# A four-segment attention and feed-forward kernel: earlier loads and tile-by-tile statistics for the third segment, another place for two loads of ScalarE, and a new table of offsets

## The chip, the cores and the metric

The kernel runs on one core of a Trainium2 chip. The core has five engines, each with an instruction queue of its own that it works through in order: TensorE (PE) for matrix products, VectorE (DVE), ScalarE (ACT), GpSimd (POOL), and SyncE (SP), which here only issues DMA transfers. Engines wait for each other through semaphores. The metric is the time of one execution on the device in microseconds; several runs are taken, and their median is quoted.

## The reference

There are 2048 tokens of width 640, 32 heads of width 20, and four segments of 512 tokens. Two layers are computed, each an attention block and a feed-forward block, both behind a layer norm and with a residual sum:

```
x = x + A(layernorm(x))
x = x + B(layernorm(x))     # relu(x @ w1) @ w2, inner width 1728
x = x + A(layernorm(x))
x = x + B(layernorm(x))

A: q, k, v = x @ wq, x @ wk, x @ wv, for 32 heads and 4 segments
   for s in range(4):
       a_dot = softmax(q_s k_s^T * scale + causal mask) v_s
       a_mem = phi(q_s) M / (phi(q_s) z + 1e-6)
       out_s = g * a_mem + (1 - g) * a_dot,     g = sigmoid(beta)
       M, z  = M + phi(k_s)^T v_s, z + sum(phi(k_s))
   return concat(out) @ wo
```

The layer norm subtracts the mean of a token's 640 values and divides by the root of their variance plus 1e-5. Before a segment's q, k and v can be projected, the statistics of its four tiles of 128 tokens must be known.

## The kernel before

The program writes no instruction order by hand. Some forty generators (streams) each describe one strand of the work: scores, exps, the causal masks, the products with v, projections, layer norms, phi, the feed-forward block, loads. A planner (class Sched) runs while the program is built. It keeps a model of when each engine is free and when each result is there, asks every stream for its next operation, and appends the one that can start first to its engine's queue. The key by which it chooses is the start time plus an offset, then a priority, then the segment. The offset comes from the table SHIFT, whose entries (stream, segment from 0 to 7 over both layers, part) give nanoseconds, negative for earlier. Durations and latencies in `dve`, `act`, `pool`, `pe` and `dma` are the planner's estimates. They alter no instruction, only the order in which instructions are put into the queues. When the program runs on the chip, the order is fixed and the semaphores decide the times.

The data goes this way. For each segment the token tiles lie in x_sb (16 tiles, a place of its own for each). `stats` (L772) makes two bn_stats of 320 columns and one bn_aggr per tile on DVE; `chain` makes the inverse root on POOL (L791); `lnorm` (L801) writes normalized tiles (L821) and has SP transpose them by DMA (`turn`, L794) into xnT, or into a part of hT for the second and third segment of the first layer. Groups of matmuls (L754 in full form, L757 in four column quarters) make q, k and v. DVE or ACT evict them out of PSUM (L961 and L962 for q and k, L1016 for v). q and k go through DRAM (scr) into the padded layout `pad`, from which PE makes the scores (L1281). ACT takes their exponentials (L1345), POOL cuts them along the diagonal (L1357), PE multiplies them with v (L1377) and the result is evicted (L1387). The products with wo, a second layer norm and the feed-forward block follow, and fill PE between the rounds of scores.

The very first segment is special. Its four tiles are loaded by `loads` (L599): tiles 0 and 1 by SP, 2 and 3 by ACT, at the start of both queues. DVE makes the statistics of tiles 0 and 1, ACT those of tiles 2 and 3 (`first_ln_b`, L887: a sum and a sum of squares, L893 to L897). They are transposed on PE (L846). `consts` (L661) lets ACT run one small exp at the start, so that its table is loaded; the same generator later makes omg and maskg from beta. `warm_pe` keeps PE busy with matmuls that nobody reads (L718). The pads of the first two head groups don't go through DRAM: `first_heads` (L1055) copies them from stg with four DMAs on SP and five on ACT (L1077).

`late_loads` (L621) is a list of pieces that SP loads later: the third segment's four tiles (the segment called 2 in the code), wo in five rows, the fourth segment's tiles, w1 in halves and w2. Each piece waits for one of the rounds of exps: piece n of the first 23 for round n*19//23, counted in fives, and all for z1 (two memsets). A name has one semaphore, whose event is set when the last piece of that name has been issued. All four tiles of a segment have one name, and `proj_ln` (L910) waits for it ahead of all four.

Of the kernel before, what the change touches and what calls it, by code (L numbers as in the profile page):

```python
# [6 lines left out]
ACT = mybir.ActivationFunctionType  # L7
ALU = mybir.AluOpType
# [4 lines left out]
DH = 20  # L13
# [5 lines left out]
G = H // 4  # L19
# [90 lines left out]
class Op:  # L110
# [4 lines left out]
    def __init__(self, alts, waits, dma=None, acq=None, urgent=False, take=(), mode="full", lag=0.0, port=False):  # L115
        self.lag = lag
        self.port = port
        self.alts = alts
        self.mode = mode
        self.cols = None  # L120
        self.cols_ns = None
        self.acq = acq
        self.waits = [t for t in waits if t is not None]
        self.dma = dma
        self.urgent = urgent
        self.take = take

# [31 lines left out]
class Spawn:  # L159
# [1565 lines left out]
```

## Time and profile before

| what | value |
|---|---|
| median of 3 runs | 554.52 us (554.39 to 555.2) |
| the profiled execution | 554.0 us |
| its span, from first to last instruction | 551.5 us |
| PE busy | 540.9 us, 98% |
| DVE busy | 421.9 us, 77% |
| ACT busy | 409.5 us, 74% |
| POOL busy | 192.0 us, 35% |
| granted clock of PE | 1.000 |

Matmuls overlap in the array, and the profile gives each its whole length. So a stretch in which PE is busy all the time can still hold short gaps between matmuls that follow each other. Where PE's busy time falls below the length of a stretch, it stood idle for certain. Rows of waits have the engine, the line and tile that waited, what ended the wait, the total in us, the number of waits, and the longest. A name with q (SPq, ACTq) is that engine's queue of DMA issues.

### The profile page before, as it was taken

Reading aid. Unit: us, or ns where it says so; the run is one execution under the profiler, and the core shown is the slowest. Engines: PE = TensorE matmul, PEld = TensorE weight load, DVE = VectorE, ACT = ScalarE, POOL = GpSimd, SP = SyncE. Lnnn points to the kernel's source line nnn. Section 1 sums busy time; section 2 is a strip of 40 time slices with the busy share of each in tenths; the row PEclk is TensorE's granted clock in tenths of the full one; section 3 lists DMA queues with packets and bytes.
Section 4 is the critical chain, followed back from the end, with each engine's and each line's share of the span. In section 5 each row is a group of like instructions: output and inputs, shape, how many; then the busy total and the mean of one; then the engine's idle time right before and its main releaser. Section 6 shows DMA issues by size and latency. Waiting matters only on the chain.

```text
span 551.5 us, 20778 instructions
## 1 busy us (share of the span) xinstructions
PE 540.9 (98%) x9171; PEld 304.7 (55%) x9171; DVE 421.9 (77%) x1057; ACT 409.5 (74%) x526; POOL 192.0 (35%) x305
## 2 busy tenths in 40 slices
PE   8998999999999999999999999999999999999998
PEld 7542554455654556545555464554556655757656
DVE  5979998898888869977998888677797889537202
ACT  6799979889777877798788978888896788441140
POOL 5345354333243324444343434443433333301000
PEclk9999999999999999999999999999999999999999
DMA  8598999844455162543775524717186331440301
GB/s 274 147 185 243 214 177 194 240 96 85 125 102 130 45 144 69 93 105 75 132 134 110 100 40 122 134 45 117 23 155 177 73 50 34 91 77 15 88 2 51
DMA packets 133325, 62.21 MB, mean 113 GB/s; under 512 B 112116, under 2 KB 123124, under 8 KB 133236
## 3 DMA queue, kind: packets, MB, share of 16 engines
q1 hardware_dynamic: 132672, 60.36, 51.0%
q8 instruction: 72, 1.18, 0.9%
q10 hardware_dynamic: 564, 0.53, 0.3%
q14 instruction: 17, 0.14, 0.1%
HBM read 20.56 MB, written 12.85 MB: 61 GB/s over the span
## 4 chain that ended last, share of the span: by engine, by line
PE 87%; DVE 5%; ACT 3%; DMA 2%; SPq 1%; POOL 1%; issue 0%
PE ps L757 35%; PE ps L754 34%; PE ps L1281 8%; PE ps L1377 6%; ACT PT L1345 3%; PE ps L1160 2%; PE ps L1218 1%; DMA oT<-o_sb 1%; PE ps L1552 1%; DVE stats L775 1%; DVE xn_tok L821 1%; DMA pad<-scr 1%; POOL rstd L791 1%; DMA x_sb<-in_A_x_dram 1%; DVE otu L1387 0%
## 5 line engine op out<-in xcount | busy, mean ns | idle before, releaser
L1345 ACT ACTIVATE PT<-ps 128x1024 bf16<-128x1024 f32 x320 | 309.3, 1026 | 66.3 <-PE ps L1281 61.0
L1357 POOL TENSOR_SCALAR_AFFINE_SELECT PT<-PT 128x512 bf16<-128x512 bf16 x256 | 165.7, 665 | 244.0 <-ACT PT L1345 243.8
L757 PE MATMUL ps<-xnT,w_r 128*32 128x512 bf16 x1340 | 81.2, 379 | 0.0
L754 PE MATMUL ps<-w_r,hT 128*128 128x320 bf16 x428 | 69.1, 300 | 0.0
L1594 DVE TENSOR_TENSOR x_sb<-x_sb,ps 128x320 bf16<-128x320 bf16 (+1 forms) x65 | 30.9, 475 | 46.0 <-PE ps L757 41.5
L1281 PE MATMUL ps<-pad 20*128 20x512 bf16 (+3 forms) x1024 | 63.4, 301 | 1.8 <-ACT PT L1345 0.9
L757 PE MATMUL ps<-w_r,hT 128*32 128x320 bf16 (+1 forms) x1668 | 64.4, 295 | 0.0
L775 DVE BATCH_NORM_STATS2 stats<-x_sb 128x6 f32<-128x320 bf16 x124 | 55.4, 475 | 3.2 <-DMA x_sb<-in_A_x_dram 2.6
L754 PEld LDWEIGHTS ps<-w_r,hT 128*128 128x128 bf16 x428 | 39.5, 98 | 19.5 <-issue 5.0
L757 PEld LDWEIGHTS ps<-xnT,w_r 128*32 128x32 bf16 x1340 | 33.2, 97 | 30.7 <-issue 2.4
L757 PEld LDWEIGHTS ps<-w_r,hT 128*32 128x32 bf16 x1668 | 42.0, 97 | 12.9 <-issue 1.6
L1575 ACT ACTIVATE hT<-ps 128x512 bf16<-128x512 f32 x54 | 32.2, 598 | 20.7 <-PE ps L757 19.7
L1281 PEld LDWEIGHTS ps<-pad 20*128 20x128 bf16 x1024 | 17.8, 92 | 53.5 <-issue 25.0
L754 PE MATMUL ps<-xnT,w_r 128*128 128x512 bf16 x185 | 45.5, 380 | 0.0
L791 POOL TENSOR_TENSOR rstd<-lnU,mhalf 128x2 f32<-128x2 f32 (+2 forms) x27 | 20.9, 774 | 67.5 <-DVE lnU L787 65.3
L1499 DVE TENSOR_TENSOR x_sb<-x_sb,ps 128x320 bf16<-128x320 bf16 x64 | 30.0, 478 | 15.5 <-PE ps L757 12.7
L1377 PE MATMUL ps<-PT,v_aug 128*21 128x128 bf16 (+3 forms) x896 | 40.3, 300 | 0.0
L1387 DVE CAST otu<-ps 128x512 bf16<-128x512 f32 x48 | 32.6, 679 | 8.4 <-PE ps L1377 8.1
L1574 DVE TENSOR_SCALAR hT<-ps 128x512 bf16<-128x512 f32 x50 | 33.9, 680 | 5.4 <-PE ps L754 3.6
L961 DVE CAST stg<-ps 128x512 bf16<-128x512 f32 (+1 forms) x44 | 29.8, 677 | 9.6 <-PE ps L754 4.8
L757 PE MATMUL ps<-wo_r,oT 128*32 128x320 bf16 x896 | 35.5, 299 | 0.6 <-DMA oT<-o_sb 0.6
L821 DVE TENSOR_SCALAR xn_tok<-x_sb,mv,rstd 128x640 bf16<-128x640 bf16 x60 | 31.1, 550 | 5.1 <-POOL rstd L791 3.5
(117 smaller groups left out, 731.3 us busy)
## 6 DMA issues: line engine op xcount, KB each, us to landing
pad<-scr SPq DMA_DIRECT2D x124, 80.0 KB
scr<-stg SPq DMA_DIRECT2D x34, 256.0 KB, 3.0
out_dram<-x_sb SPq DMA_DIRECT2D x15, 160.0 KB, 1.8
w_r<-in_B_w_dram SPq DMA_DIRECT2D x10, 216.0 KB, 3.0
w_r<-in_B_w_dram SPq DMA_DIRECT2D x13, 160.0 KB, 3.0
x_sb<-in_A_x_dram SPq DMA_DIRECT2D x10, 160.0 KB, 3.7
scr<-w_r SPq DMA_DIRECT2D x5, 256.0 KB, 3.3
wv_r<-in_A_wv_dram SPq DMA_DIRECT2D x1, 800.0 KB, 8.7
```

What stands on the lines that cost most here:

```text
L754: return e.matmul(view(dst.ap, b), a, b, start=(k == 0), stop=(k == last))
L757: return e.matmul(view(dst.ap[rows], b), part, b, start=(k == 0), stop=(k == last))
L775: tk = yield dve(320, 1, lambda e, c2=c2: e.bn_stats(stats6[:, t, c2, :], x_sb[:, t, c2 * 320:(c2 + 1) * 320]), xt)
L821: nm = lambda e, bx, t, k: e.tensor_scalar(bx.ap[:, k * D:k * D + D], x_sb[:, t + k, :], mv[:, t + k, 0:1], rstd[:, t + k:t + k + 1], ALU. ...
L1281: fns.append([(lambda e, z=z, j=j, hh=hh, N=N, o=o, sl=sl, q=hh % 2: e.matmul(slot.ap[:, q, o:o + N], sl.ap[32 * hh:32 * hh + DH, z, 0, 12 ...
L1345: tx = yield act(1024, lambda e, dst=dst, src=src: e.activation(dst, src, ACT.Exp, scale=SCALE), sc + pw)
L1357: tm = yield pool(600.0, lambda e, reg=reg: e.affine_select(out=reg, in_=reg, pattern=[[0, 4], [1, 128]], compare_op=ALU.is_ge, fill=0.0, ...
L1377: fns.append((lambda e, OD, j=j, hh=hh: e.matmul(OD.ap[32 * hh:32 * hh + DH + 1, 128 * j:L], VAUG[vx(a, s)][:, j, 4 * g + hh, :], pt.ap[:, ...
L1387: te = yield evac(L, 1, lambda e: e.tensor_copy(dst, OD.ap), lambda e: e.activation(dst, OD.ap, ACT.Copy), [tk] + OTU[0].tks)
L1574: th = yield evac(512, 1, lambda e: e.tensor_scalar(hT[:, dc, :], bk.ap[:, :], 0.0, None, ALU.max), lambda e: e.activation(hT[:, dc, :], b ...
L1575: lambda e: e.activation(hT[:, dc, :], bk.ap[:, :], ACT.Relu), [tk] + HT.tks)
L1594: ta = yield dve(n, 1, lambda e: e.tensor_tensor(x_sb[:, t, c0:c0 + n], x_sb[:, t, c0:c0 + n], bk.ap[:, 0:n], ALU.add), [tk], urgent=True)
```

## The change

Five things change.

The pieces of the third and fourth segment's tiles get a name, a semaphore and an event for each tile, and `proj_ln` waits for tile i ahead of tile i's statistics.

The third segment's four pieces no longer wait for a round of exps or for z1: they come when `first_heads` has put its transfers into the queues. The other pieces keep their gates; the wait for z1 is taken up from the fifth piece on.

In `loads`, the loads of tiles 2 and 3 on ACT come after the small exp of `consts` in ACT's queue. That exp is preceded by the load of ACT's table.

In the planner, a DVE operation that shares a port with POOL is no longer held until POOL is free plus 150 ns. The planner now remembers the last operations of both engines, and lengthens one by the overlap with the other. The copy of omg and the products for maskg count as such operations. Latencies of some transfers are raised: 2700 for wk and wq in place of 2000, 2200 in place of 1500 for the first heads' pads, 2900 in place of 2400 for the transposes of o.

The table of offsets is another one: 267 entries before, 242 after, with one entry alike.

```
@@ SHIFT
-    (0, 0, 0): -201, (0, 7, 1): -12, (1, 0, 0): 400, (1, 0, 1): 400, (1, 0, 2): 400, (1, 1, 0): -275, (1, 1, 1): -225,
...
+    (1, 0, 0): -50, (1, 0, 1): -100, (1, 2, 0): 225, (1, 2, 1): 625, (1, 2, 2): 500, (1, 3, 0): 100, (1, 3, 1): -75,
...
@@ _alts
-            if e == "dve" and op.port and self.free["pool"] > start:
-                hold = max(hold, self.free["pool"] - start + PORT_NS)
+            if e == "dve" and op.port:
+                for a, b in self.held["pool"][-6:]:
+                    if a <= start + 66.0 < b:
+                        hold = max(hold, b - start + op.data - 70.0)
+            if e == "pool":
+                for a, b in self.held["dve"][-6:]:
+                    if a < start + hold and b > start:
+                        hold = hold + b - max(a, start)
@@ run
+            if e == "dve" and op.port:
+                self.held[e].append((end - op.data, end))
+            elif e == "pool":
+                self.held[e].append((start, end))
@@ ld
-            tk = yield dma(e, sem_("d_" + name), nbytes, fn, waits, lat=1470.0 if name[:2] == "x0" else 2000.0)
+            tk = yield dma(e, sem_("d_" + name), nbytes, fn, waits, lat=1470.0 if name[:2] == "x0" else 2700.0 if name[:2] in ("wk", "wq") else 2000.0)
@@ loads
             for t in range(4):
+                if t == 2:
+                    yield Need("warmed")
                 yield from ld(("sp", "act")[t // 2], "x0%d%d" % divmod(t, 2), 163840, lambda e, t=t: e.dma_start(
                     x_sb[:, t, :], xs[:, t, :]))
@@ late_loads
-                return [("x%d" % s, 163840, one(4 * s + i)) for i in range(4)]
+                return [("x%d%d" % (s, i), 163840, one(4 * s + i)) for i in range(4)]
...
-            z1 = yield Need("z1")
+            z1 = []
...
-                w = yield Need("ex", *divmod(25 + (n - n2) // 2 if n >= n2 else n * 19 // n2, 5))
+                if name[:2] == "x2":
+                    yield Need("direct", 0)
+                    w = []
+                else:
+                    w = yield Need("ex", *divmod(25 + (n - n2) // 2 if n >= n2 else n * 19 // n2, 5))
+                if n == 4:
+                    z1 = yield Need("z1")
@@ consts
-            yield act(4, lambda e: e.activation(warm[:], warm[:], ACT.Exp), [tw], psum=False)
+            ta = yield act(4, lambda e: e.activation(warm[:], warm[:], ACT.Exp), [tw], psum=False)
+            S.set("warmed", tks=[ta])
...
@@ proj_ln
-                xw = [[("x10",)]] * 2 + [[("x11",)]] * 2 if s == 1 else [[("x%d" % s,)]] * 4
+                xw = [[("x10",)]] * 2 + [[("x11",)]] * 2 if s == 1 else [[("x%d%d" % (s, i),)] for i in range(NJ)]
@@ first_heads
-                            sl.ap[p0:p0 + rb - ra, z], stg[ra - 128 * c:rb - 128 * c, c]), ev + sl.tks, issue=720.0, rate=200.0)
+                            sl.ap[p0:p0 + rb - ra, z], stg[ra - 128 * c:rb - 128 * c, c]), ev + sl.tks, issue=720.0, lat=2200.0, rate=200.0)
```

More of the change, by code (lines that the diff above doesn't have):

```diff
@@ L126, in __init__ @@
         self.take = take
+        self.data = 0.0
 class Slot:
@@ L240, in __init__ @@
         self.made = {}
+        self.held = {"dve": [], "pool": []}
     def add(self, prio, gen):
@@ L465, in mm_ns @@
     return max(26.0, n / 2.4 + 2.6)
-PORT_NS = 150.0
 def dve(n, mode, fn, waits=(), extra=0.0, acq=None, urgent=False, port=False):
-    return Op([("dve", 66.0 + n / (0.96 * mode) + extra, [(fn, True)], 95.0)], waits, acq=acq, urgent=urgent,
-              port=port or mode > 1)
+    op = Op([("dve", 66.0 + n / (0.96 * mode) + extra, [(fn, True)], 95.0)], waits, acq=acq, urgent=urgent,
+            port=port or mode > 1)
+    op.data = n / (0.96 * mode)
+    return op
 def act(n, fn, waits=(), psum=True):
@@ L703, in consts @@
             to = yield dve(32, 1, lambda e: e.tensor_copy(
-                omg[:], gt[:, 1, :].rearrange("p (g hh) -> p g hh", g=G)), [tr])
+                omg[:], gt[:, 1, :].rearrange("p (g hh) -> p g hh", g=G)), [tr], port=True)
             S.set("omg", tks=[to])
@@ L710, in consts @@
                 tm = yield dve(140, 1, lambda e, mc=mc, h0=h0, h1=h1: e.tensor_tensor(
-                    mc, mc, gt[:, 2, h0:h1][:, :, None].to_broadcast([128, h1 - h0, DH]), ALU.mult), [tg] + tmm)
+                    mc, mc, gt[:, 2, h0:h1][:, :, None].to_broadcast([128, h1 - h0, DH]), ALU.mult), [tg] + tmm, port=True)
                 tms.append(tm)
@@ L792, in chain, with turn @@
             return tk
-        def turn(slot_sem, dst, src, waits):
+        def turn(slot_sem, dst, src, waits, lat=2400.0):
             n = src.shape[-1] // 128
             tk = yield dma("sp", slot_sem, 32768 * n, lambda e: e.dma_start_transpose(dst, src), waits,
-                           issue=max(1400.0, 140.0 * n), lat=2400.0, rate=270.0, holds=True)
+                           issue=max(1400.0, 140.0 * n), lat=lat, rate=270.0, holds=True)
             return tk
@@ L1510, in turn_o @@
                 tT = yield from turn(ot_sem[id(ot)], ot.ap, o_sb[:, 2 * k:2 * k + 2, :].rearrange(
-                    "p i d -> p (i d)"), ow + ot.tks)
+                    "p i d -> p (i d)"), ow + ot.tks, 2900.0)
                 turned.append(tT)
```

82 rows, old and new, of the table SHIFT are left out of this document.

## The prediction

> **What bounds the kernel now.** I read the page first, then the busy time by stretch, the waits of PE, the chain that ended last, and the timelines of the start and of SP's queue. The profiled execution took 554.0 us: a span of 551.5 and 2.5 around it. The median of the runs shown is 554.52, 0.5 above it; I add my sum to the median. A difference under 0.2%, 1.1 us, can't be told from no change here.
>
> The page's busy shares: time, share of the span, instructions.
>
> ```profile
> PE 540.9 (98%) x9171; PEld 304.7 (55%) x9171; DVE 421.9 (77%) x1057; ACT 409.5 (74%) x526; POOL 192.0 (35%) x305
> ```
>
> PE leaves 10.6 us of the span open. The stretches say where (start:end and length, then busy us of PE, weight loads, DVE, ACT, POOL, then clock, DMA share, GB/s):
>
> ```profile
> 0.00:10.00 10.00, 7.79 (x88) 6.97 (x89) 5.41 (x17) 5.95 (x15) 4.17 (x16) 1.00 0.82 253
> 10.00:20.00 10.00, 9.84 (x86) 6.88 (x84) 7.38 (x24) 5.73 (x14) 4.08 (x12) 1.00 0.52 158
> 15.00:20.00 5.00, 4.87 (x35) 2.84 (x33) 4.67 (x16) 2.39 (x3) 0.08 (x1) 1.00 0.26 57
> 20.00:30.00 10.00, 9.43 (x79) 4.35 (x80) 9.84 (x24) 8.68 (x12) 4.89 (x7) 1.00 0.92 208
> 30.00:40.00 10.00, 9.52 (x169) 5.03 (x157) 6.75 (x15) 9.64 (x12) 5.08 (x8) 1.00 0.95 189
> 40.00:50.00 10.00, 8.11 (x109) 2.99 (x112) 9.83 (x26) 9.55 (x12) 4.84 (x8) 1.00 0.92 237
> 50.00:60.00 10.00, 9.08 (x119) 3.67 (x110) 9.26 (x21) 9.59 (x12) 6.52 (x10) 1.00 0.94 208
> 80.00:480.00 400.00, 399.41 (x6440) 218.06 (x6441) 331.12 (x823) 327.68 (x406) 152.60 (x234) 1.00 0.51 106
> 480.00:551.50 71.50, 69.13 (x1808) 45.48 (x1799) 23.51 (x60) 16.48 (x29) 1.52 (x2) 1.00 0.22 48
> ```
>
> From 80 to 480 PE shows 0.59 us of idle time; the last 71 us are feed-forward on PE alone, and no edit touches them. So only the first 60 to 80 us have visible idle time. From 20 to 30 and from 40 to 60 DVE is as good as full, while from 30 to 40 it has 3.25 us free (10.00 less 6.75). PE's idle time from 40 to 60 is 1.89 + 0.92 = 2.81 us. The waits of PE between 20 and 80 name DVE first:
>
> ```profile
> PE ps L754 <- DVE otu L1387: 1.6, 3, 0.7
> PE ps L757 <- DVE v_aug L1016: 1.2, 2, 0.6
> PE ps L1281 <- DMA pad<-scr: 0.6, 1, 0.6
> ```
>
> Both DVE rows are evictions of PSUM that stood in DVE's queue behind other work. What that work was, the chain that ended last shows:
>
> ```profile
> 31.52 12.92 ACT PT L1345 x14
> ...
> 47.55 0.41 DVE stats L775
> ...
> 47.99 0.21 DVE mv L777
> ```
>
> These are statistics of the third segment's token tiles (8 to 11). The timeline has their first and last pairs, and then the first of the fourth segment (start, length, engine, line):
>
> ```profile
> 40.60 0.87 DVE L775 BATCH_NORM_STATS2 stats<-x_sb 128x6 f32<-128x320 bf16 x2
> 48.12 0.83 DVE L775 BATCH_NORM_STATS2 stats<-x_sb 128x6 f32<-128x320 bf16 x2
> 57.41 0.88 DVE L775 BATCH_NORM_STATS2 stats<-x_sb 128x6 f32<-128x320 bf16 x2
> ```
>
> They stand that late because of their loads, which SP's queue shows (the last row is the fourth segment's):
>
> ```profile
> 12.99 3.19 SPq L1077 DMA_DIRECT2D pad<-stg  x4
> 19.25 0.36 SPq L625 DMA_DIRECT2D x_sb<-in_A_x_dram  x1
> ...
> 21.91 0.33 SPq L625 DMA_DIRECT2D x_sb<-in_A_x_dram  x1
> 34.46 0.42 SPq L625 DMA_DIRECT2D x_sb<-in_A_x_dram  x1
> 41.40 1.85 SPq L625 DMA_DIRECT2D x_sb<-in_A_x_dram  x4
> ```
>
> Three tiles are asked for by 22 us, the fourth at 34.46, and one semaphore covers all four: nothing of this segment can start before the fourth has landed.
>
> **The change, part by part.**
>
> *A. The third segment's loads.* No instruction is added: four DMAs move on SP, three from between 19.25 and 21.91 and one from 34.46, to right behind the four first-head transfers, which end at 16.18 (12.99 + 3.19). Each holds SP for about 0.4 us, so they stand from 16.2 to 17.8, in a gap that lasts to 19.25. Nothing that SP issues later is pushed. DMA share is 0.26 from 15 to 20, so the 640 KB meet little. An issue of this load takes a median of 3.7 us to land, by the row
>
> ```profile
> x_sb<-in_A_x_dram SPq DMA_DIRECT2D x10, 160.0 KB, 3.7
> ```
>
> so the tiles are there from 19.9 to 21.5 in place of about 38.2 (34.46 + 3.7). With a semaphore for each tile, the statistics can be laid into any hole from 20 us on. They are eight instructions of 475 ns and four of 0.21: 4.6 us of DVE.
>
> ```profile
> L775 DVE BATCH_NORM_STATS2 stats<-x_sb 128x6 f32<-128x320 bf16 x124 | 55.4, 475 | 3.2 <-DMA x_sb<-in_A_x_dram 2.6
> ```
>
> DVE's hole from 30 to 40 takes 3.25 us of that, and the evictions between 40 and 60 move up. The most that this gives is PE's whole idle time there with the 0.48 of 30 to 40, 3.29 us; the least is nothing, since ACT is 9.5 to 9.6 full from 30 to 60 and sets the pace of the scores. I take 2.8 less a part for what is late next: 2.4. Late next is the transfer of the second segment's first pads (the 0.6 us in the waits of PE), which waits for DMA and gains nothing. Two transposes of this segment, the first on SP at 53.02 before, move up in SP's queue too, past the pad loads and a transpose of otu. Each takes about 1.35 us:
>
> ```profile
> 53.02 1.34 SPq L797 DMA_TRANSPOSE hT<-xn_tok  x1
> ```
>
> What stands behind one on SP comes that much later; four pad slots cover it, and if they don't, a score round waits up to 1.35 us. I charge nothing and keep 1.35 for the range. The fourth segment's loads keep their gates and their place in the list; their statistics already came long after the last of them (issued by 43.25, used from 57.41), so tile-by-tile waits give nothing there. Six more semaphores carry waits on DVE, no work. The wait on z1 now stands ahead of the fifth piece, the first row of wo, and comes from two memsets at the very start: nothing.
>
> *B. ScalarE's two x loads.* Now they go first; in the new order the table load and the small exp precede them. The rows, of ACT's queue, ACT and PE:
>
> ```profile
> 0.80 0.90 ACTq L608 DMA_DIRECT2D x_sb<-in_A_x_dram  x2
> 1.73 1.28 ACT L663 ACT_TABLE_LOAD   x1 [1.73 <-PEq L1710]
> 3.03 0.20 ACT L663 ACTIVATE warm<-warm 128x1 f32<-128x1 f32 x1
> 3.87 0.74 ACT L893 ACTIVATE hT<-x_sb 128x640 bf16<-128x640 bf16 x1 [0.64 <-DMA x_sb<-in_A_x_dram]
> 7.60 0.19 ACT L897 ACTIVATION_READ_ACCUMULATOR hT<-x_sb,mv 128x1 f32 x1
> 8.17 0.55 POOL L791 TENSOR_TENSOR rstd<-lnU,mhalf 128x1 f32<-128x1 f32 x1
> 10.24 0.44 PE L846 MATMUL ps<-om_sb,xn_tok 128*128 128x128 bf16 x5
> 11.27 0.39 PE L754 MATMUL ps<-xnT,wk_r 128*128 128x256 bf16 x2
> ```
>
> The table load can start at about 0.83 and end at 2.11, the exp at 2.33, so the loads go out from 2.33. Tile 2 took 3.07 us from issue to ACT's first use (0.80 to 3.87): it would be used at 5.40. The two tiles' sums on ACT take 3.92 us (3.87 to 7.79) and end at 9.32 in place of 7.79, 1.53 later. From there the chain needs rstd (ready at 8.72), the normalized tile, its transposes and a copy. Tile 3's transposes ran at 10.24 though they could have at about 9.2: PE was busy with tile 1's projections. That 1.04 us of slack takes up most, and the 256-column projections of 11.27 come 0.5 later. The high end is a load that shares with wk and wq, issued by SP from 1.72:
>
> ```profile
> wk_r<-in_A_wk_dram SPq DMA_DIRECT2D x1, 320.0 KB, 4.3
> ```
>
> With 4.3 us to land, tile 2 is there at 6.63 and the projections come 1.7 later. I take 0.8: the tile is half the size of that weight piece, so nearer the low end. A gain is excluded: the projections of 11.27 feed the first heads and wait for tile 3, and PE has nothing else there, as wv lands at 4.25 + 8.7 = 12.95.
>
> ```profile
> wv_r<-in_A_wv_dram SPq DMA_DIRECT2D x1, 800.0 KB, 8.7
> ```
>
> PE is 9.84 full right after, so these 0.8 us stay to the end. That SP's own two tiles may land sooner, alone on the wire, gives nothing while tile 3 sets the start.
>
> The Trainium skill, "DMA: Bandwidth & Descriptors", section on queues, rings and completion order, says that each DMA engine goes round its queues a packet at a time, and that SP and ACT own one queue each. By that the late x tiles get a share at once rather than wait for all of wk, and the sum keeps the low end; what the late issue costs remains. The trace bears it out so far: tiles issued by both queues at 0.80 were used at 3.67 and 3.87. The skill's "ScalarE: Activation LUTs", on what ACT_TABLE_LOAD costs, adds a drain of 1.38 us to the 1.28 of the load; with it the loads would go out at 3.7 and B would cost about 1.9. The trace shows no such drain, as the exp starts 0.02 us after the load ends, so I keep 2.33.
>
> *C. The planner's costs and the offsets.* The costs of DVE operations beside POOL and the latencies of some transfers are numbers of the planner; with the new table of offsets (267 entries before, 242 after, one alike) they change only the order on each engine. Their place is 80 to 480, with no visible PE idle time to win. What an order can change there lies under the overlap of matmuls: weight loads that wait for ACT before a score round.
>
> ```profile
> PEld ps L1281 <- ACT PT L1345: 23.2, 57, 1.1
> ```
>
> Of these 6.2 us in 15 waits fall between 20 and 80, so 17.0 in 42 waits outside:
>
> ```profile
> PEld ps L1281 <- ACT PT L1345: 6.2, 15, 1.1
> ```
>
> As an estimate an order wins or loses up to a sixth of that, 2.8 us, to either side. I take -0.4, near the middle: the copy of omg at 26.23 took 0.61 us for 32 columns beside POOL, and a planner that knows of such lengthenings places DVE's work a little better.
>
> ```profile
> 26.23 0.61 DVE L703 COPY omg<-gt 128x32 f32<-128x32 f32 x1
> ```
>
> **Sum.** -2.4 (A) + 0.8 (B) - 0.4 (C) = -2.0: 554.5 becomes 552.5.
>
> **Rivals.**
>
> *The order wins more.* The third segment's projections, ready some 15 us earlier, fill the hidden gaps too, and C is at its good end: -3.3 + 0.5 - 2.8 = -5.6, or 549. For it speaks that PE ran only 112 weight loads from 40 to 50, against 157 in the ten microseconds before; against it that DVE and ACT must still evict what PE makes, and ACT has 0.4 us free in 10.
>
> *Hidden anyway.* ACT's row of fourteen exps (12.92 us without a gap) sets the pace from 31 to 44, the moved statistics only shift DVE's queue, and A gives nothing. Then B alone remains: 554.5 + 0.8 = 555.3, within the measurement.
>
> *Slower: the statistics stand in front of evictions.* DVE is 9.84 full from 20 to 30, just where the tiles now land. If the order puts all of them there, 4.6 us of work goes in front of evictions that PE waits for. What DVE wins back later is at most 3.25, its hole. With B, 4.6 - 3.25 + 0.8 = 2.2: 556.7. It decides from the point where more than 1.6 us of statistics (three or four of the eight instructions) run before 30 us: with 2.4 from A less 0.8 of B, that eats the gain. For it speaks that the planner starts whatever can start first; against it that evictions come ahead of statistics at equal times (they are marked urgent).
>
> **How the numbers follow.** The forecast has 0.38, with a range of its own of 550.8 to 553.4; the order that wins more 0.16; hidden anyway 0.14; slower 0.32. Faster by over 0.2% is the first two, 0.54; within 0.2% 0.13, the hidden case but for a hundredth; slower the rest, 0.33. The range leaves out one in ten at each end: 548.0, a microsecond below the good rival, and 557.5, since the slower one with B at its high end and 1.35 for a late pad load would be 558.9, and I cut its last part.
>
> **What would show it.** A: the third segment's statistics run between 20 and 40 us, DVE has under 1.5 us free from 30 to 40, and PE idles under 1 us from 40 to 60. It is wrong if PE idles longer before 30 with DVE's evictions as the releaser. B: ACT's table load starts before 1.0, its first sum at 5.4 or later, the 256-column projections at about 12.0; if they stay at 11.3, B is free. C: from 80 to 480 PE still has under 1 us idle, and the waits of weight loads for ACT stay near 23 us; beyond 26, or below 20, the order has decided more than A and B. The prediction fails if the gap between the runs is there only after 80 us.

## The result, and the profile after

The changed kernel takes 553.6 us (median of 22 runs, 552.57 to 555.34). The kernel before, run beside it, takes 554.56 (553.81 to 555.97). The ratio is 0.9981, with an interval of 0.9973 to 0.9989: faster by 1.0 us, where 2.0 were forecast. The profiled span went from 551.5 to 550.7.

The busy shares of the changed kernel:

```profile
PE 542.5 (98%) x8958; PEld 304.3 (55%) x8958; DVE 426.4 (77%) x1056; ACT 409.2 (74%) x527; POOL 192.5 (35%) x305
```

The stretches of the changed kernel, with the same columns as in the prediction:

```profile
0.00:20.00 20.00, 17.55 (x165) 13.08 (x166) 12.59 (x39) 10.55 (x28) 8.05 (x26) 1.00 0.79 236
20.00:80.00 60.00, 58.42 (x760) 28.82 (x759) 57.72 (x143) 55.85 (x69) 29.85 (x44) 1.00 0.97 217
80.00:480.00 400.00, 398.11 (x6246) 216.93 (x6247) 332.27 (x815) 326.58 (x405) 153.21 (x233) 1.00 0.50 103
```

and of the kernel before in the same three cuts:

```profile
0.00:20.00 20.00, 17.64 (x170) 13.85 (x171) 12.79 (x41) 11.68 (x28) 8.25 (x27) 1.00 0.67 206
20.00:80.00 60.00, 54.76 (x765) 27.32 (x763) 54.47 (x135) 53.65 (x66) 29.64 (x44) 1.00 0.94 207
80.00:480.00 400.00, 399.41 (x6440) 218.06 (x6441) 331.12 (x823) 327.68 (x406) 152.60 (x234) 1.00 0.51 106
```

Between 20 and 80 us PE idles 60.00 - 58.42 = 1.58 us instead of 5.24. Not only PE: DVE does 3.25 us more in these 60, and ACT 2.20 more. Between 80 and 480 a part goes the other way: 1.89 us idle instead of 0.59. The visible idle time falls by more than the span does, because a matmul is shown at its whole length and short gaps hide beneath overlaps. So these columns say where PE stood still, in this one execution; what that is worth, only the runs say. In a second profile of the changed kernel PE idles 2.24 us between 20 and 80.

The waits of PE between 20 and 80, in the changed kernel:

```profile
PE ps L770 <- DVE otu L1403: 0.5, 1, 0.5
PE ps L1393 <- DVE v_aug L1032: 0.4, 1, 0.4
PE ps L770 <- DVE v_aug L1032: 0.2, 1, 0.2
```

The waits for otu and v_aug, 2.8 us before, are 1.1 now. The third segment's loads and its statistics, from the timeline:

```profile
16.23 2.30 SPq L634 DMA_DIRECT2D x_sb<-in_A_x_dram  x4
...
26.60 0.48 DVE L791 BATCH_NORM_STATS2 stats<-x_sb 128x6 f32<-128x320 bf16 x1
27.59 0.48 DVE L791 BATCH_NORM_STATS2 stats<-x_sb 128x6 f32<-128x320 bf16 x1
28.89 0.83 DVE L791 BATCH_NORM_STATS2 stats<-x_sb 128x6 f32<-128x320 bf16 x2
30.74 0.83 DVE L791 BATCH_NORM_STATS2 stats<-x_sb 128x6 f32<-128x320 bf16 x2
32.51 0.83 DVE L791 BATCH_NORM_STATS2 stats<-x_sb 128x6 f32<-128x320 bf16 x2
```

The statistics run between 26.6 and 33.3, and other DVE work stands between them; before they ran from 40.6 to 49.0. And the start:

```profile
0.80 1.28 ACT L678 ACT_TABLE_LOAD   x1 [0.80 <-PEq L1726]
1.15 0.90 ACTq L617 DMA_DIRECT2D x_sb<-in_A_x_dram  x2
2.09 0.20 ACT L678 ACTIVATE warm<-warm 128x1 f32<-128x1 f32 x1
3.83 0.74 ACT L909 ACTIVATE hT<-x_sb 128x640 bf16<-128x640 bf16 x1 [1.54 <-DMA x_sb<-in_A_x_dram]
10.97 0.71 PE L770 MATMUL ps<-xnT,wk_r 128*128 128x256 bf16 x5
```

The second row belongs to ACT's queue of DMA issues. It lies inside the first one: the loads go out at 1.15, while the table load runs until 2.08. So tile 2 is used at 3.83, as early as before (3.87).

### The profile page after: what moved, and what is told of

Same layout as the page of the kernel before. It is cut to its first block, busy times and chain, and to the rows that moved or that the text cites. A ratio compares the mean times of both kernels' runs of the same rounds, so it can differ in the third digit from the quotient of the medians.

```text
span 550.7 us, 20357 instructions
## 1 busy us (share of the span) xinstructions
PE 542.5 (98%) x8958; PEld 304.3 (55%) x8958; DVE 426.4 (77%) x1056; ACT 409.2 (74%) x527; POOL 192.5 (35%) x305
## 3 DMA queue, kind: packets, MB, share of 16 engines
q8 instruction: 70, 1.15, 0.8%
## 4 chain that ended last, share of the span: by engine, by line
PE 80%; DVE 12%; DMA 4%; SPq 1%; ACT 1%; POOL 1%; issue 0%
PE ps L773 33%; PE ps L770 30%; PE ps L1297 7%; PE ps L1393 6%; DVE stats L791 2%; DVE xn_tok L837 2%; PE ps L1176 2%; DMA x_sb<-in_A_x_dram 1%; DMA oT<-o_sb 1%; DVE o_sb L1487 1%; DVE otu L1403 1%; DMA otk<-otu 1%; DVE w_r L977 1%; PE ps L1234 1%; ACT PT L1361 1%; DMA scr<-stg 1%
## 5 line engine op out<-in xcount | busy, mean ns | idle before, releaser
L773 PE MATMUL ps<-xnT,w_r 128*32 128x512 bf16 x1332 | 80.0, 379 | 0.0
L773 PE MATMUL ps<-w_r,hT 128*32 128x320 bf16 (+1 forms) x1796 | 69.3, 295 | 0.0
L770 PE MATMUL ps<-w_r,hT 128*128 128x320 bf16 x396 | 63.7, 300 | 0.0
L1591 ACT ACTIVATE hT<-ps 128x512 bf16<-128x512 f32 x47 | 28.1, 599 | 35.4 <-PE ps L773 35.0
L773 PEld LDWEIGHTS ps<-w_r,hT 128*32 128x32 bf16 x1796 | 45.0, 97 | 13.2 <-issue 1.1
L1590 DVE TENSOR_SCALAR hT<-ps 128x512 bf16<-128x512 f32 x57 | 38.8, 683 | 13.7 <-PE ps L773 11.5
L770 PEld LDWEIGHTS ps<-w_r,hT 128*128 128x128 bf16 x396 | 36.6, 98 | 18.7 <-issue 5.5
L1487 DVE TENSOR_TENSOR o_sb<-otk,rden 128x320 bf16<-128x320 bf16 x62 | 33.7, 572 | 0.5
L1142 ACT ACTIVATE stg<-stg 128x512 bf16<-128x512 bf16 x50 | 31.8, 637 | 2.6 <-DVE rtmp L1140 2.6
```

The lines of the kernel that those rows point to most:

```text
L770: return e.matmul(view(dst.ap, b), a, b, start=(k == 0), stop=(k == last))
L773: return e.matmul(view(dst.ap[rows], b), part, b, start=(k == 0), stop=(k == last))
L1142: te = yield act(512, lambda e, q=q: e.activation(q, q, ACT.Exp), [tr] + p, psum=False)
L1487: to = yield dve(320, 1, lambda e, z=z, dst=dst: e.tensor_tensor(dst, av[:, z, :, :, 0:DH], rd.ap[:, z].to_broadcast([128, NJ, 4, DH]), AL ...
L1590: th = yield evac(512, 1, lambda e: e.tensor_scalar(hT[:, dc, :], bk.ap[:, :], 0.0, None, ALU.max), lambda e: e.activation(hT[:, dc, :], b ...
```

## Experiments

Theory, after the result: the gain is made before 80 us, by the early tiles (A) in DVE's hole, B costs nothing, and the order after 80 us does little. Rivals: B wins or loses something; the loads alone win; the new order wins with or without the early tiles; the later order gives gains back.

For most experiments the program carries a list of the planner's choices, recorded from one kernel, and follows it instead of choosing. That holds the order on every engine still while one part is changed:

```
@@ run
-            _, st, end, start, k, op = best
+            uid, k0, mode0 = PLAN[len(self.log)]
+            hit = [h for h in heads if self.uid[id(h[2][1])] == uid]
+            _, _, st, alts, op, _ = hit[0]
+            end, start, k, _ = [a for a in alts if a[2] == k0][0]
```

**B alone, in the kernel before.** Only ACT's two loads move behind its table load.

```
@@ loads
+                if t == 2:
+                    yield Need("warmed")
@@ consts
-            yield act(4, lambda e: e.activation(warm[:], warm[:], ACT.Exp), [tw], psum=False)
+            ta = yield act(4, lambda e: e.activation(warm[:], warm[:], ACT.Exp), [tw], psum=False)
+            S.set("warmed", tks=[ta])
```

> The kernel before with part B alone: ScalarE's two x loads stand behind the small exp; every other instruction keeps its place. Theory, from the two traces: ACT's queue sends the loads while its table load still runs, so they go out only 0.35 us later, the tiles of SP land 0.5 us sooner, and the 256-column projections start at about 11.0 in place of 11.27; the time falls by 0 to 0.3 us. Rival, my prediction's step B: the loads go out at 2.33, the projections start 0.5 to 1.7 later, and the time rises by about 0.8 us.

Measured: 554.65 us against 555.17, ratio 0.9996 [0.9988, 1.0005]. Its timeline:

```profile
0.80 1.28 ACT L665 ACT_TABLE_LOAD   x1 [0.80 <-PEq L1713]
0.97 0.86 ACTq L610 DMA_DIRECT2D x_sb<-in_A_x_dram  x2
2.09 0.20 ACT L665 ACTIVATE warm<-warm 128x1 f32<-128x1 f32 x1
3.83 0.74 ACT L896 ACTIVATE hT<-x_sb 128x640 bf16<-128x640 bf16 x1 [1.54 <-DMA x_sb<-in_A_x_dram]
11.05 0.72 PE L757 MATMUL ps<-xnT,wk_r 128*128 128x256 bf16 x5
```

The issue comes 0.17 us later than before, not 1.53, and the projections at 11.05 come no later than at 11.27. The start of one trace varies by more than this step (the last section has the numbers), so the runs decide: their interval excludes a loss of 0.8 us (1.0014).

**The changed kernel without B.** The gate of the first diff is taken out of `loads` again.

```
@@ loads
-                if t == 2:
-                    yield Need("warmed")
```

> The changed kernel with part B undone: the two x loads are first in ScalarE's queue again; nothing else moves. Theory: 0 to 0.3 us slower than the changed kernel, so about 553.7. Rival, step B of the prediction: 0.8 us faster, about 552.8.

Measured: 553.22 us, 0.9968 [0.9954, 0.9981]. That can't be told from the changed kernel, so B isn't where the gain comes from either.

**The early loads alone.** The order of the kernel before; only the third segment's four loads move on SP to behind the first heads' transfers, with a semaphore for each.

```
@@ late_loads
-                return [("x%d" % s, 163840, one(4 * s + i)) for i in range(4)]
+                return [("x%d%d" % (s, i), 163840, one(4 * s + i)) for i in range(4)]
...
+                if name[:2] == "x2":
+                    yield Need("direct", 0)
+                    w = []
```

> The kernel before in its own order of instructions, with only the third segment's four loads moved on SP to right behind the first heads' transfers and a semaphore for each tile; the statistics stay where they were on DVE. Theory: early landing alone wins nothing, since DVE reaches the statistics at 40 us as before: within 0.6 us of the kernel before. Rival: taking four transfers out of the stretch from 19 to 38 us lets pads and transposes land sooner: 1 us or more faster.

Measured: 555.05 us, 1.0002 [0.9992, 1.0012]. Tiles that are there earlier win nothing while their statistics stay where they were.

**A by hand, in the order before.** Beside the early loads, the third segment's eight bn_stats and four bn_aggr move in the list to VectorE's hole between 30 and 40 us, and the inverse root and the first normalized tiles to where the statistics stood. PE's order is the old one.

```
@@ PLAN (VectorE, third segment)
-  ... o_sb, bn_stats, bn_aggr, ..., bn_stats, bn_aggr, xn_tok
+  bn_stats, bn_aggr (tiles 8 to 11, from 33.9 to 41.8 us), ..., xn_tok (43.8 us)
```

> The order of the kernel before with the early loads, and with the third segment's statistics moved by hand into the stretch of 30 to 40 us on DVE, its root and normalized tiles to where the statistics stood; PE's order is the old one. Theory: DVE's evictions between 40 and 60 come earlier and PE's idle time there falls from 2.8 us to 1.5 or less; without a new order on PE half of the gain of part A, 1 us, is left: 0.998. Rival: ACT sets the pace until 60 us, so the time stays within 0.5 us.

Measured: 555.44 us, 1.0004 [0.9993, 1.0016]. No gain, although the hole is filled. The theory, 0.998, is refuted. The rival's time fits, but not its reason, since ACT, which was to set the pace, is busy for less than before between 40 and 60 (18.07 us instead of 19.14). Two stretches of 20 us tell why; first of the kernel before, then of this one, then of the changed kernel:

```profile
20.00:40.00 20.00, 18.95 (x240) 9.38 (x237) 16.59 (x38) 18.32 (x23) 9.97 (x15) 1.00 0.94 198
40.00:60.00 20.00, 17.18 (x220) 6.66 (x220) 19.09 (x46) 19.14 (x22) 11.36 (x17) 1.00 0.93 223
```

```profile
20.00:40.00 20.00, 19.00 (x224) 9.56 (x221) 19.16 (x50) 18.32 (x23) 9.41 (x14) 1.00 0.87 186
40.00:60.00 20.00, 16.04 (x215) 6.10 (x208) 15.93 (x34) 18.07 (x21) 10.41 (x16) 1.00 0.90 230
```

```profile
20.00:40.00 20.00, 19.61 (x224) 9.36 (x226) 19.43 (x51) 19.23 (x25) 10.49 (x15) 1.00 0.91 191
40.00:60.00 20.00, 18.82 (x304) 7.88 (x304) 18.78 (x42) 20.00 (x23) 12.07 (x19) 1.00 1.04 258
```

DVE's third number is 16.59 and 19.09 before, 19.16 and 15.93 by hand. The sums are 35.68 and 35.09: the hole was not used, it went 20 us further on, and PE has 3.96 us idle behind it instead of 2.82. In the changed kernel DVE has 38.21 us of work in the same 40. The execution profiled by hand came to its first projections 1.22 us late (12.49 instead of 11.27). That isn't what moved the hole: the kernel with the early loads alone was as late in its profile (12.26), and DVE has 16.70 and 18.73 us there, with PE idle for 2.52 behind.

What ended DVE's idle time in the hole of the kernel before, 30 to 40 us, is on record too:

```profile
DVE otu L1387 <- PE ps L1377: 1.0, 1, 1.0
DVE M_sb L1233 <- PE ps L1218: 0.8, 1, 0.8
DVE w_r L961 <- PE ps L754: 0.5, 1, 0.5
DVE v_aug L1016 <- PE ps L757: 0.4, 1, 0.4
DVE v_aug L1016 <- PE ps L754: 0.2, 1, 0.2
```

In 2.9 of the 3.25 us DVE waited for a result of PE. By hand it waits for PE again, for 2.8 us between 40 and 60, and 1.1 us for the inverse root. So the free time of DVE was no place that waited for work. It was what was left when PE had made too few results for DVE to evict. The wait that took the place of the old one shows in the timelines of DVE and PE of the kernel by hand:

```profile
43.79 1.41 DVE L917 TENSOR_SCALAR xn_tok<-x_sb,mv,rstd 128x640 bf16<-128x640 bf16 x2 [1.13 <-POOL rstd L887]
```

```profile
45.66 0.61 PE L853 MATMUL ps<-hT,wk_r 128*32 128x512 bf16 x8 [1.32 <-DVE v_aug L1112]
```

An eviction (v_aug) stood in DVE's queue behind two normalized tiles, which had themselves waited for the inverse root.

What PE has on its list in the two kernels shows in its groups of K projections of the second and third segment together, from 0 to 80 us. Before:

```profile
L754 PE MATMUL ps<-hT,wk_r 128*128 128x512 bf16 x20 | 5.5, 380 | 1.2 <-DVE otu L1387 1.2
L757 PE MATMUL ps<-hT,wk_r 128*32 128x512 bf16 x48 | 3.7, 382 | 0.6 <-DVE v_aug L1016 0.6
```

and in the changed kernel:

```profile
L770 PE MATMUL ps<-hT,wk_r 128*128 128x512 bf16 x47 | 12.7, 380 | 0.1
L773 PE MATMUL ps<-hT,wk_r 128*32 128x512 bf16 x12 | 0.8, 382 | 0.0
```

Four of the 32-column form make one full product. So of the two segments' 50 the kernel before has made 20 + 12 = 32 by 80 us, and the changed kernel 47 + 3 = 50. It is more than an exchange: of Q both have made 30 from hT, of V 80 before and 74 now. The third segment's K projections, counted in order, run from 57.29 to 66.81 us in the changed kernel, and from 62.00 to 87.48 in the kernel before. By hand PE made 20 + 10 of K by 80 us; early statistics that no projection uses earlier won nothing there.

**The changed order for 88 us, then the old one.** All edits are in. The first 900 choices (to about 88 us) are those of the changed kernel; what is then left follows in the order of the kernel before.

```
@@ PLAN
+PLAN = AFTER[:900] + rest(BEFORE, AFTER[:900])
```

> The order of the changed kernel for its first 900 planned steps (to about 88 us), and from there on the order of the kernel before, for all that is still to be done. Theory: the start of the changed kernel wins about 2.3 us, and its order after 80 us loses 1.3 to 1.9 of them again; with the old order there the time is about 552.3, 1.0 to 1.5 below the changed kernel. Rival: the two stretches don't belong together and what the start wins is lost at the seam, or the start wins only 1 us in the first place: 553.5 or more.

Measured: 552.87 us, 0.9966 [0.9953, 0.9978]. The whole gain is there with the old order from 88 us on, so the edits and the new order of the first 88 us are enough for it. The theory expected more, 552.3, since the old order would win back the 1.3 us more that PE idles behind 88; that lies just outside the interval, 552.6 to 553.9. The rival's 553.5 or more is inside it. On the same chip the changed kernel without B, with the new order to the end, had 0.9968, so the old order behind 88 us wins nothing that these runs resolve.

**The changed order for 205 us.** The same with the first 2000 choices.

```
@@ PLAN
+PLAN = AFTER[:2000] + rest(BEFORE, AFTER[:2000])
```

> The order of the changed kernel for its first 2000 planned steps (to about 205 us), then the order of the kernel before. Theory that the order of the changed kernel gives back some 0.8 us evenly after 88 us: about 0.9973, between the splice at 88 us (0.9966) and the changed kernel (0.9981). Rival, that one place between 205 and 480 us loses it: 0.9966 or lower. Rival, that the loss lies between 88 and 205: 0.998.

Measured: 554.76 us, 0.9995 [0.9979, 1.0010]: the gain is gone. The stretch where the two lists meet, and the last one, of this kernel:

```profile
200.00:260.00 60.00, 59.95 (x811) 32.93 (x811) 48.04 (x123) 39.96 (x51) 19.26 (x30) 1.00 0.42 89
```

```profile
480.00:554.00 74.00, 69.81 (x1824) 46.64 (x1812) 23.50 (x60) 16.89 (x29) 1.52 (x2) 0.99 0.22 47
```

PE has no stall at the joint (0.05 us idle). ACT shows it: 39.96 us busy in these 60, against 47.90 in the changed kernel and 48.68 before, because the new order has ACT ahead by then (99.12 us from 88 to 200, against 93.00 before). That this costs the gain isn't shown. In the last stretch PE has 69.81 us of work left, 1.4 more than the changed kernel (68.38 from 480 us on), but the splice at 88 us has 69.36. The two splices were profiled in executions of 555.17 and 554.54 us, closer together than their medians, 554.76 and 552.87, so their traces can't show the place. The interval reaches from a gain of 0.2% to a loss of 0.1%, and just clears that of the splice at 88 us. So the order behind 88 us can lose the gain, though the whole new order doesn't. Where this kernel loses what the splice at 88 us keeps isn't settled; neither the theory nor its two rivals had a place for it.

**The changed kernel once more,** on the chip of the splice at 205 us, with no edit.

> The changed kernel itself, beside the others of this group on the same chip: 0.998 of the kernel before, as in its own runs. Its first 20 us may lie a microsecond apart between executions, since the second tile of ScalarE landed at 6.10 here and at 6.71 in a run with the same start.

Measured: 553.62 us against 554.99, 0.9964 [0.9951, 0.9977]. With the first result, 0.9981, the gain is between 1.0 and 2.0 us.

**The first scores earlier.** The changed kernel starts its scores later than the kernel before (19.17 against 17.77 us). In this one the first round moves ahead of one group of projections on PE, and its exp ahead of one eviction on ACT.

```
@@ PLAN (PE, about 18 us)
-  projection group, scores of round 0
+  scores of round 0, projection group
```

> The changed kernel with the first round of scores one matmul group earlier on PE, and its exp ahead of one eviction on ACT; nothing else moves. The trace of the changed kernel has the first scores at 19.17 without a wait for their pads, and the kernel before at 17.77. Theory: the pads are there by 18.2, the first exp starts some 0.8 us earlier, and up to 60 us, where ACT is full, the gain stays: 0.3 to 0.8 us faster than the changed kernel. Rival: the pads land no sooner and PE waits for them, 0.2 to 0.6 us slower.

Measured: 553.44 us, 0.9973 [0.9957, 0.9988], the same as the changed kernel. In its profile the first scores stand at 19.17 again, because its first projections came 0.86 us later than in the changed kernel's (11.83 instead of 10.97); counted from them the scores are 0.86 us earlier. The 0.3 to 0.8 us of the theory aren't seen. Whether scores that are really earlier on the clock would win, one trace can't say.

**The old order fitted to A, and its control.** The kernel by hand left it open that A lacks only an order of its own. Here single choices are moved between 13 and about 100 us wherever the planner's own estimate of the end falls, once with the early tiles (a_refit), once in the kernel before without any of the edits (before_refit).

```
@@ PLAN (a_refit, before_refit)
-  choice i
...
+  choice i, moved up or down among choices 150 to 1000
```

> The order of the kernel before, with the third segment's four x loads behind the first heads' transfers, its statistics tile by tile, ScalarE's loads as they were, and then single pieces of work moved along their engines between 13 and about 100 us until the early tiles are used. Theory (the 2.2 us that the changed kernel lost fewer of between 20 and 80 us come from early tiles together with an order around them): ratio to before 0.996 to 0.9985, PE idle in 40 to 60 us under 1.2 us (2.8 before), and it is faster than its control before_refit by 0.5 to 2 us. Rival (any other fit of the order of the first 100 us wins as much, the tiles have nothing to do with it): the same ratio here, and the same in before_refit.

> Control: the kernel before, its loads and its statistics in one sweep where they were, and only single pieces of work moved along their engines in the same way and in the same stretch. Theory: ratio to before 0.9985 to 1.0015, because VectorE's hole between 30 and 40 us cannot be filled before the third segment's tiles are there; PE idle in 40 to 60 us stays at 2 us or more. Rival: 0.996 to 0.9985, and the hole's cost is gone without the early tiles.

Measured: a_refit 555.9 us against 554.88, 1.0009 [0.9998, 1.0020]; before_refit 554.47, 0.9993 [0.9982, 1.0003]. The theory expected 0.996 to 0.9985 of the first, and that is refuted. The control came out as the theory said in time, though its idle time from 40 to 60 us, 1.87, is a little under the bound of 2. From 20 to 80 us PE idles 3.38 us in the control instead of 5.24, and that won nothing which the runs resolve: less visible idle time in this stretch is no gain by itself. The stretches of a_refit:

```profile
20.00:80.00 60.00, 54.38 (x743) 26.64 (x745) 54.13 (x133) 53.51 (x65) 28.09 (x42) 1.00 0.92 199
80.00:480.00 400.00, 399.28 (x6421) 217.73 (x6417) 334.23 (x827) 327.44 (x405) 153.67 (x236) 1.00 0.51 106
```

PE idles 5.62 us from 20 to 80, as before. And its list has stayed the old one: from 0 to 80 us it makes 20 + 10 K projections, as by hand.

```profile
L859 PE MATMUL ps<-hT,wk_r 128*128 128x512 bf16 x20 | 5.6, 380 | 1.2 <-DVE otu L1492 1.2
L862 PE MATMUL ps<-hT,wk_r 128*32 128x512 bf16 x40 | 3.1, 383 | 0.3 <-DVE w_r L1066 0.3
```

Moves of one choice at a time didn't bring the third segment's projections forward. So this run says that A gains nothing in the neighbourhood of the old order. It doesn't say that no other order than the changed kernel's can use it.

**The changed kernel, fitted in the same way.** The same moves, in the changed kernel's list.

```
@@ PLAN (after_refit)
-  choice i
...
+  choice i, moved up or down
```

> The changed kernel with single pieces of work moved along their engines in the same way, all its parts in place. If the order still leaves something in the first 100 us: 0.995 to 0.997 against before, that is 0.3 to 1 us under the changed kernel. If the changed kernel's order is as good as this kind of moving makes it: 0.997 to 0.999, the same as the changed kernel.

Measured: 556.97 us, 1.0034 [1.0022, 1.0046]. Slower than both kernels, which neither expectation had. Its stretch from 80 to 480 us has lost most:

```profile
80.00:480.00 400.00, 396.70 (x6150) 214.86 (x6151) 324.02 (x808) 327.97 (x405) 152.92 (x233) 1.00 0.52 103
```

PE idles 3.30 us there, against 1.89. The moves were chosen for a lower estimate of the planner, and the chip took 3 us or more longer than for the changed kernel: at this size the estimate didn't say which of the two orders is faster. That holds for the two fits before as well, so they are weaker evidence than the kernel by hand.

**The new code with the old offsets.** The planner chooses again, with the early loads, the tile-by-tile waits and B, but with the costs and the table of the kernel before.

```
@@ SHIFT
-    (1, 0, 0): -50, (1, 0, 1): -100, (1, 2, 0): 225, ...
+    (0, 0, 0): -201, (0, 7, 1): -12, (1, 0, 0): 400, ...
@@ _alts
+            if e == "dve" and op.port and self.free["pool"] > start:
+                hold = max(hold, self.free["pool"] - start + PORT_NS)
```

> The new code (early loads, statistics tile by tile, ScalarE's loads behind the table load) with the old costs and offsets of the heads, so that the order written out is another one. Theory (offsets belong to one order each, they win nothing by themselves but cost much when they do not fit): slower than before by 5 to 15 us, ratio 1.01 to 1.027, the idle time of PE spread over 80 to 480 us and not in the first 80. Rival (the offsets are fine tuning worth under 1 us): 0.997 to 1.001.

Measured: 570.13 us, 1.0271 [1.0247, 1.0294], slower by 15.3 us.

```profile
20.00:30.00 10.00, 8.65 (x97) 3.97 (x97) 9.60 (x26) 8.99 (x12) 4.83 (x7) 1.00 0.73 137
30.00:40.00 10.00, 7.40 (x99) 3.58 (x91) 8.00 (x21) 7.60 (x11) 3.78 (x6) 1.00 0.94 219
...
80.00:480.00 400.00, 390.82 (x6090) 210.61 (x6092) 326.92 (x810) 322.87 (x400) 151.84 (x230) 1.00 0.50 102
```

PE idles 9.18 us from 80 to 480, where it had 0.59 before, so most of the visible loss is spread there, as expected. But 20 to 40 us lose too, 3.95 against 1.05, which was not. The same edits that gain 1 to 2 us with a table and costs made for them lose 15 with those of the kernel before. Which of the two, table or costs, weighs more, this run doesn't part.

## Why the prediction was right or wrong

*The time.* 552.5 was forecast, 553.6 measured: inside the range and with the sign right, but 0.2 us above the likeliest case's own range, which ended at 553.4, and half of the forecast change. A gain of 0.19% lies in the class within 0.2%, which was given 0.13; the 0.36% of the second group of runs lies in the class of a faster kernel, which was given 0.54. The three terms behind it fared worse than their sum.

*A, -2.4.* The place fits: the new order of the first 88 us is enough for the gain, as the splice shows. Its signs came, the last nearly: the statistics run between 20 and 40 us (26.6 to 33.3), DVE has 0.22 us free from 30 to 40 (the bound was 1.5), and PE idles 1.18 us from 40 to 60, where under 1 was asked. The fault is in the step "the statistics can be laid into any hole from 20 us on ... and the evictions between 40 and 60 move up". By hand that was done, with the statistics from 33.9 to 41.8 us, and nothing was gained: the hole moved on. The step took DVE's free time for a cause; it was a consequence of what PE had to do. What the traces point to in its place is that PE gets work earlier: in the changed kernel it has all of the third segment's K projections by 80 us. That is a matter of PE's order, which the prediction put under C and after 80 us. That these projections carry the gain is argued from the counts; no run moves them alone. So the total came near by luck: A as described wins nothing, the order of the first 88 us that wins was not in the sum, and B's loss, which pulled the other way, isn't there.

*B, +0.8.* Refuted, and by its own sign: the 256-column projections came at 10.97, not at 12.0. The failed step is "the loads go out from 2.33": it took ACT's queue of DMA issues to wait for the table load and the exp. Measured, the issue lies inside the table load, 0.17 and 0.35 us later than before, and B alone gave 0.9996. Here the trace of before could have warned little: in it the loads stood ahead of the table load, so it showed what the issues cost the table load (1.73 instead of 0.80), not the reverse. The bound from below, "a gain is excluded", was sound reasoning from a wrong start, and nothing turned on it.

*C, -0.4, between 80 and 480.* Its size can't be told from nothing, and its place was wrong. From 88 us on the old order does as well (0.9966 against 0.9981 and 0.9964). Of its two signs one failed, as PE idles 1.89 us from 80 to 480 and not under 1. The other, the waits of weight loads for ACT in the whole span, went from 23.2 to 26.0, just to the bound beyond which the order was to have decided:

```profile
PEld ps L1297 <- ACT PT L1361: 26.0, 66, 0.7
```

From 80 to 480 us alone, these waits were the following before, in the changed kernel, and in the splice at 88 us:

```profile
PEld ps L1281 <- ACT PT L1345: 16.9, 42, 0.4
```

```profile
PEld ps L1297 <- ACT PT L1361: 20.9, 52, 0.7
```

```profile
PEld ps L1388 <- ACT PT L1452: 17.4, 41, 1.4
```

Between the second and the third lie 3.5 us of such waits and no difference in time that the runs resolve. So a sixth of them was no measure of what an order can win. What an order can win or lose is shown by the other runs: 1 to 2 us won with the new order of the first 88, that gain lost again with the splice at 205 us, 15 us lost with a table and costs that don't fit.

*The rivals.* The statistics in front of evictions: its condition came true, four of the eight bn_stats, 1.79 us, ran before 30 us (26.60 to 29.72). Yet PE was busy without a gap then:

```profile
20.00:30.00 10.00, 10.00 (x113) 5.25 (x115) 9.64 (x25) 9.45 (x13) 4.34 (x6) 1.00 0.85 154
```

So its point of decision was wrong: statistics that stand between evictions in this order delayed none that PE needed before 30 us. The mechanism itself exists, though, with normalized tiles in the place of statistics: it is the 1.32 us wait of the kernel by hand. "Hidden anyway" is what happens when only A is made (1.0002, 1.0004), though for another reason than ACT's pace. "The order wins more" named the right carrier, the third segment's projections filling PE, and gave it some three to six times its size (5.6 against 1.0 to 2.0 us).

*Open.* Whether the order of the first 88 us would win without the early tiles wasn't tried: its statistics at 26.6 us would stand on DVE waiting for loads that land at about 38, so the order can't be run as it is with the old loads. So the early tiles are shown not to be enough; that they are needed is only argued, and one trace speaks in part against it. In the kernel before, the third segment's last transpose is issued at 56.75 us and takes 1.35, and its first K projections run at 62.00, but only 7 of its 25 by 80. In the changed kernel they start at 57.29, not 5 us sooner, and all 25 are done by 66.81. Most of that step lies in PE's list; whether it can be had with the old loads and late statistics stays open.

## What to carry to other kernels

An idle stretch of an engine that isn't the bound need not be a place to be filled: look at what ended its idle time, ask whether the bound engine gets work sooner if it is filled, and look for that work in the bound engine's own list. An earlier load is worth what the bound engine's order makes of it, so test the load and the order apart, by replaying one recorded order. And a table of tuned offsets belongs to one program: judged with the old table and costs, these edits would have looked like a loss of 15 us.

## What the runs showed of the hardware

ACT's queue issues DMAs while ACT's table load runs: the issues stand at 0.97 and 1.15 us inside a load from 0.80 to 2.08. The Trainium skill, "ScalarE: Activation LUTs", on what ACT_TABLE_LOAD costs, gives the load 1283 ns, which agrees with the 1.28 us here; that a DMA issue behind it goes out meanwhile, the trace alone shows.

The first 20 us vary between executions, by more than a microsecond, for two reasons that the traces show. One is when loads land: in a second profile of the changed kernel PE stood 0.49 us at 8.90 waiting for wq, which it didn't in the first, and the 256-column projections of the first segment came at 11.33 instead of 10.97. The other is PE's own speed. In the profiles of the kernel by hand and of the splice at 88 us the granted clock was 0.50 from 8 to 10 us, and five matmuls of 128 columns took 0.74 us, where they take 0.44 in the kernel before and in the changed one. The stretch of the splice at 88 us:

```profile
8.00:10.00 2.00, 2.00 (x21) 2.00 (x20) 0.98 (x3) 0.89 (x3) 0.74 (x2) 0.50 1.09 353
```

There the projections came at 12.49 and 12.52, against 11.27 before and 10.97 in the changed kernel. With the early loads alone five such matmuls took 0.74 us as well, and the projections came at 12.26, though its profile gives a clock of 1.00 in that stretch. A step of a microsecond at the start can't be read from one trace.
